# A gated recurrence followed by a two-matrix network: natural-order 64-column output tiles, whole loads of w_in, decays and operands one step ahead, three double-bank PSUM tiles

## The chip, the cores and the metric

The kernel runs on one core of a Trainium2 chip. The metric is device time in microseconds (us); the span that a profile shows is 1 to 2 us shorter. Runs called slow are left out of every comparison unless the text says so.

The engines are named as in the profile: PE is TensorE (PEld its weight loads), DVE is VectorE, ACT is ScalarE, POOL is GpSimd, SP issues the DMAs. `L142` is line 142 of the kernel that the profile belongs to.

## The reference

```python
batch, n_heads, seq, head_dim = (4, 8, 768, 48)
for t in range(S):                                     # _attn_ref(q, k, v, alpha)
    state = alpha[:, :, t, :, None] * state + np.einsum('bhd,bhe->bhde', k[:, :, t], v[:, :, t])
    y[:, :, t] = np.einsum('bhd,bhde->bhe', q[:, :, t], state)
# x = y as 3072 tokens x 384;  w_in is 384 x 2048, w_out is 2048 x 384
h = x @ w_in
g = h * np.cos(h)
out = g @ w_out
```

The inputs and the output are float32. The kernel works on 24 chunks of 128 tokens, six per batch entry, in bfloat16 with float32 sums.

## The kernel before

For each chunk the kernel does this, under the names that the text uses:

- **ln, sums, exps**: `ln` of alpha on ACT, cumulative sums by matmuls with a triangle of ones, then `exp(-sum)` (icp) and `exp(sum)` (cp) on ACT. All three are done for two chunks at a time.
- **operands**: POOL multiplies k by icp (khb) and q by cp (qhb), and casts v.
- **transposes** of khb and qhb on PE, evicted by DVE.
- **scores** (8 matmuls) with a mask on DVE; **state** (matmuls of khb and v plus the old state), evicted with the decay by DVE; **outputs** (old state and scores against v), evicted by DVE as the transposed x.
- **ff1**: 48 matmuls per chunk in two halves of 24. Each half fills one PSUM tile of two banks. ACT takes the cosine of the tile (`Sin` with a bias), and the **gate** on DVE multiplies.
- **ff2**: 16 matmuls, evicted by ACT and stored.

Step `s` of the loop runs ff1 of chunk `s`, ff2 of `s-1`, outputs of `s+1`, and transposes, state and scores of `s+2`. The order of instructions on each engine is the order of the program. The parts that matter, cut:

```python
    ps = ctx.enter_context(tc.tile_pool(name="ps", bufs=2, space=bass.MemoryType.PSUM))
    # tags: "big" [C,2,512] f32 = two banks (sums, scores, ff1); "g" one bank (transposes, state,
    # outputs); "o" one bank (ff2). Two buffers of each: 4 + 2 + 2 = 8 banks.

    def load_w1(f0, f1):                     # rows of w_in permuted to the order of outputs' rows
        w = moe_w_in[:, f0:f1].rearrange("(p a d) f -> a d p f", a=2, d=D)
        for i in range(2):
            nc.sync.dma_start(out=w1f[DA * i : DA * i + DA, :, f0:f1], in_=w[i, 0:DA, 0:3])
            nc.sync.dma_start(out=w1f[96:128, i, f0:f1], in_=w[i, 0:DA, 3])
        for i in range(2):
            o = 64 + DB * i
            nc.sync.dma_start(out=w1f[o : o + DB, :, f0:f1], in_=w[i, DA:D, 0:3])
            nc.sync.dma_start(out=w1f[o + 32 : o + 32 + DB, 2, f0:f1], in_=w[i, DA:D, 3])
    # ... cut ...
    # outputs(j): 28 matmuls into 32-column tiles, four of them side by side (16 in the first chunk
    # of a batch entry, where there is no state)
    # ... cut ...
    for s in range(NCH + 1):
        # ... loads for later steps, cut ...
        if s == 0:
            cums(2, 2); exps(2, 2); operands(2)
        elif s + 2 < NCH:
            operands(s + 2)
        if s + 2 < NCH:
            transposes(s + 2); ev_transposes(s + 2)
        if s < NCH:
            ff1(s, 0); t0 = act(s, 0)
        if s + 2 < NCH:
            state(s + 2); ev_state(s + 2)
        if s < NCH:
            gate(s, 0, t0)
        # ... casts of w_out in step 1, cut ...
        if s >= 1:
            ff2(s - 1, 0)
        if s < NCH:
            ff1(s, 1); t1 = act(s, 1)
        if s + 1 < NCH:
            outputs(s + 1); ev_outputs(s + 1)
        if s < NCH:
            gate(s, 1, t1)
        if s >= 1:
            ff2(s - 1, 1)
        if s + 2 < NCH:
            scores(s + 2); mask_scores(s + 2)
        if s % 2 == 0 and s + 4 < NCH:
            ln(s + 4, 2)
        if s % 2 == 1 and s + 3 < NCH:
            cums(s + 3, 2); exps(s + 3, 2)
        if s >= 1:
            ev_ff2(s - 1)
```

## Time and profile before

| what | value | where it is read |
|---|---|---|
| time, median of the first 3 runs | 290.99 us | times |
| span, mean granted TensorE clock | 289.8 us, 0.859 | cores |
| PE, DVE, ACT, POOL busy | 74, 48, 50, 26 % of the span | page, part 1 |
| DMA share, 0 to 50 us | 0.96 to 1.14 | windows of 10 us |
| ff1 of step 2 starts | 69.65 us | timeline |
| ff1 of step 20 starts, nine pairs of steps later | 256.66 us | timeline |
| table loads on ACT | 21+10+10+1 = 42, 1283 ns each | groups by line |

The page of the kernel before, part 2, cuts the span into 40 slices of 7.25 us. Digits are tenths (9 is 90% or more); the last row is GB/s.

```profile
PE   7402191695976958959949949959769769769995
PEclk9955568577997997998988979979969959979999
DMA  9999999904266157347525633642660650500001
GB/s 148 193 161 164 204 368 173 168 0 102 39 138 134 45 99 136 78 63 136 111 61 104 138 71 67 138 106 40 130 136 3 139 110 9 105 27 29 29 29 54
```

There are two regimes. For the first eight slices DMA is full and PE has little to do. DMA moves 148 to 204 GB/s while it loads w_in and the inputs, and 368 GB/s in the sixth slice, where w_out loads. From about 60 us on, PE is busy but for a dip every third slice or so, and the granted clock dips with it.

The waits of the kernel before say what the dip is (who waited for whom: us in total, times, longest):

```profile
POOL khb L184 <- ACT icp_new L172: 163.8, 12, 16.1
PE t L212 <- POOL khb L184: 50.7, 13, 9.1
PE t L212 <- POOL qhb L186: 4.9, 13, 0.6
```

And so does the chain of waits of the kernel before, in a window over one dip (start, duration, what):

```profile
105.79 0.09 PE cum_new L159 x4
...
106.09 1.15 issue
107.25 0.81 ACT icp_new L172
108.06 0.71 ACT cp_new L174
...
109.18 0.97 POOL qhb L186
110.15 0.05 issue
110.20 0.61 PE t L212 x4
110.81 2.32 PE t L320 x24
...
114.76 1.34 PE t L320 x24
```

The sums end, a table loads (the 1.15 us called issue), two exps run, POOL makes khb and qhb, and only then does PE transpose and start ff1. PE is idle for 3.4 us. Its next 24 ff1 matmuls take 2.32 us where the same 24 take 1.34 us later on: the granted clock is 0.50 to 0.60 over the first ff1 half after each of these dips. This comes once in two steps, ten times in all.

### The profile page before, as it was taken

What the parts mean: (1) busy time and instruction counts of PE and PEld (TensorE: products, weight loads), DVE (VectorE), ACT (ScalarE), POOL (GpSimd) and SP (SyncE); (2) the same over time, 40 slices, a digit from 0 to 9 for tenths busy, and PEclk for the clock granted to TensorE, in tenths of its full rate; (3) what the DMA queues carried; (4) which work ended last, traced back from release to release, by engine and by line L of the source; (5) the groups of instructions that cost most, each with busy time, mean ns of one, the idle gap of its engine ahead of it and who ended that gap; (6) DMA issues with size and microseconds to landing.
All of it is one profiled execution on the core that took longest, in us unless ns stands there. A gap on an engine that the chain in (4) does not pass through costs nothing.

```text
span 289.8 us, 6578 instructions
## 1 busy us (share of the span) xinstructions
PE 213.9 (74%) x2798; PEld 161.6 (56%) x2798; DVE 139.6 (48%) x162; ACT 145.8 (50%) x153; POOL 75.7 (26%) x178
## 2 busy tenths in 40 slices
PE   7402191695976958959949949959769769769995
PEld 2201081464755737738737747647557557557782
DVE  3333333651762653643735726717616616617651
ACT  4100345116755853863864666567555556553332
POOL 4131133007108007026034052071080080080000
PEclk9955568577997997998988979979969959979999
DMA  9999999904266157347525633642660650500001
GB/s 148 193 161 164 204 368 173 168 0 102 39 138 134 45 99 136 78 63 136 111 61 104 138 71 67 138 106 40 130 136 3 139 110 9 105 27 29 29 29 54
DMA packets 106463, 30.32 MB, mean 105 GB/s; under 512 B 100545, under 2 KB 105665, under 8 KB 106433
## 3 DMA queue, kind: packets, MB, share of 16 engines
q1 hardware_dynamic: 106432, 29.89, 52.5%
q8 instruction: 22, 0.36, 0.5%
q14 instruction: 9, 0.07, 0.1%
HBM read 25.17 MB, written 4.72 MB: 103 GB/s over the span
## 4 chain that ended last, share of the span: by engine, by line
PE 58%; SPq 9%; ACT 7%; DMA 7%; DVE 7%; issue 6%; POOL 4%; POOLq 0%; ACTq 0%; DVEq 0%
PE t L320 26%; PE o_new L343 18%; DVE g_new L334 5%; DMA w1f<-in_moe_w_in_dram 5%; PE t L212 4%; PE t L296 4%; POOL qhb L186 4%; ACT icp_new L172 3%; SPq L100 3%; ACT cp_new L174 2%; SPq L110 2%; DMA t<-in_k_dram 2%; SPq L105 2%; PE cum_new L155 2%; DVE t L304 2%
## 5 line engine op out<-in xcount | busy, mean ns | idle before, releaser
L329 ACT ACTIVATE c_sb<-t,halfpi 128x1024 bf16<-128x1024 f32 x48 | 53.5, 1114 | 81.7 <-PE t L320 81.5
L320 PE MATMUL t<-t,w_114 128*128 128x128 bf16 x1152 | 86.6, 242 | 0.1
L320 PEld LDWEIGHTS <-w_114 128*128 128x128 bf16 x1152 | 82.0, 111 | 3.9 <-issue 0.7
L343 PE MATMUL o_new<-w_116,g_new 128*128 128x384 bf16 x384 | 72.8, 335 | 2.7 <-DVE w_116 L136 2.7
L184 POOL TENSOR_TENSOR khb<-t,icp_new 128x384 bf16<-128x384 f32 x24 | 24.6, 1023 | 183.0 <-ACT icp_new L172 163.8
L334 DVE TENSOR_TENSOR g_new<-t,c_sb 128x1024 bf16<-128x1024 f32 x48 | 58.8, 1224 | 15.8 <-ACT c_sb L329 15.3
L343 PEld LDWEIGHTS <-g_new 128*128 128x128 bf16 x384 | 36.3, 100 | 27.0 <-issue 5.5
L212 PE MATMUL t<-ident_bf,khb 128*128 128x128 bf16 x96 | 12.0, 263 | 50.7 <-POOL khb L184 50.7
L218 DVE COPY t<-t 128x1024 bf16<-128x1024 bf16 x24 | 16.5, 687 | 60.1 <-PE t L212 60.1
L212 PEld LDWEIGHTS <-khb 128*128 128x128 bf16 x96 | 6.9, 114 | 53.4 <-POOL khb L184 52.3
L238 DVE TENSOR_TENSOR t<-t,mask_f 128x1024 bf16<-128x1024 f32 x24 | 29.3, 1223 | 0.0
L264 DVE TENSOR_TENSOR t<-t,Em 128x384 bf16<-128x384 f32 x24 | 13.4, 558 | 31.6 <-PE t L258 22.2
L329 ACT ACT_TABLE_LOAD x21 | 26.9, 1283 | 0.4
L304 DVE CAST t<-t 128x384 bf16<-128x384 f32 x24 | 13.4, 557 | 23.1 <-PE t L296 23.1
L186 POOL TENSOR_TENSOR qhb<-t,cp_new 128x384 bf16<-128x384 f32 x24 | 23.9, 998 | 0.1
L142 ACT ACTIVATE lnab<-a_new 128x768 bf16<-128x768 f32 (+1 forms) x13 | 10.3, 794 | 26.5 <-DMA a_new<-in_alpha_dram 24.7
L172 ACT ACT_TABLE_LOAD x10 | 12.8, 1283 | 20.7 <-PE cum_new L159 20.7
L155 PE MATMUL cum_new<-lnab,triu_bf 128*128 128x384 bf16 x24 | 7.7, 348 | 11.8 <-ACT lnab L142 10.1
L212 PE MATMUL t<-ident_bf,qhb 128*128 128x128 bf16 x96 | 12.2, 267 | 4.9 <-POOL qhb L186 4.9
L142 ACT ACT_TABLE_LOAD x10 | 12.8, 1283 | 3.4 <-DMA a_new<-in_alpha_dram 3.2
L296 PE MATMUL t<-t,vpb 128*32 128x128 bf16 x192 | 14.2, 219 | 0.0
L348 ACT ACTIVATE o_sb<-o_new 128x384 f32<-128x384 f32 x24 | 11.7, 487 | 5.0 <-PE o_new L343 5.0
(48 smaller groups left out, 184.2 us busy)
## 6 DMA issues: line engine op xcount, KB each, us to landing
a_new<-in_alpha_dram SPq DMA_DIRECT2D x24, 192.0 KB, 3.3
t<-in_k_dram SPq DMA_DIRECT2D x24, 192.0 KB, 3.7
t<-in_q_dram SPq DMA_DIRECT2D x24, 192.0 KB, 4.0
t<-in_v_dram SPq DMA_DIRECT2D x24, 192.0 KB, 4.1
out_dram<-o_sb SPq DMA_DIRECT2D x24, 192.0 KB, 2.0
w2f<-in_moe_w_out_dram SPq DMA_DIRECT2D x4, 768.0 KB, 8.9
w1f<-in_moe_w_in_dram SPq DMA_DIRECT2D x4, 384.0 KB, 6.6
w1f<-in_moe_w_in_dram SPq DMA_DIRECT2D x4, 192.0 KB, 9.2
```

The source lines that it names most:

```text
L142: nc.scalar.activation(out=lnab[:, g % 2, lo : lo + n, :, 0:D], in_=a_t[g][:, lo : lo + n], func=AF.Ln)
L172: nc.scalar.activation(out=icp_t[g][:, lo : lo + n], in_=cum_ps[g][:, lo : lo + n, 0:HD], func=AF.Exp, scale=-1.0)
L184: nc.gpsimd.tensor_tensor(out=khb[:, j % 2, :, 0:D], in0=k_sb, in1=icp.rearrange("s (h d) -> s h d", h=H), op=ALU.mult)
L186: nc.gpsimd.tensor_tensor(out=qhb[:, j % 2, :, 0:D], in0=q_sb, in1=cp[:, 0:HD].rearrange("s (h d) -> s h d", h=H), op=ALU.mult)
L212: nc.tensor.transpose(t[:, (i * NP + p) * C : (i * NP + p + 1) * C], src[:, j % 2, 2 * p : 2 * p + 2].rearrange("s h d -> s (h d)"), ident_bf)
L238: nc.vector.tensor_tensor(out=t.rearrange("s (h t) -> s h t", h=H), in0=A_ps.pop(j).rearrange("s (h t) -> s h t", h=H), in1=mask_f.unsquee ...
L296: nc.tensor.matmul(t[32 * qd : 32 * qd + 32, kt * C : (kt + 1) * C], w, m, start=(r == 0), stop=(r == len(mms[qd]) - 1), skip_group_check= ...
L304: nc.vector.tensor_copy(out=t.rearrange("r k t -> r (k t)"), in_=y_ps.pop(j)[:, 0 : 3 * C])
L320: nc.tensor.matmul(t[:, f], w1[:, kk, ft * C : (ft + 1) * C], x_t[j][:, kk], start=(kk == 0), stop=(kk == 2))
L329: nc.scalar.activation(out=c_sb, in_=t, func=AF.Sin, bias=halfpi, scale=1.0)
L334: nc.vector.tensor_tensor(out=g_t[j][:, half * HF : (half + 1) * HF], in0=t, in1=c_sb, op=ALU.mult)
L343: nc.tensor.matmul(o_ps[j][:, 0:DM], g_t[j][:, ft], w2[:, ft], start=(ft == 0), stop=(ft == NF - 1))
```

## The change

The intent: outputs come out in the natural order of the rows of x, in tiles of 64 columns, so that w_in loads in whole DMAs; decays and operands are prepared one step earlier; PSUM holds three double-bank tiles and one buffer each of the small ones. The core of the diff, cut:

```diff
-    ps = ctx.enter_context(tc.tile_pool(name="ps", bufs=2, space=bass.MemoryType.PSUM))
+    ps = ctx.enter_context(tc.tile_pool(name="ps", bufs=1, space=bass.MemoryType.PSUM))
     ... every tile of tag "big" gets bufs=3; khb and qhb get three slots instead of two
     def load_w1(f0, f1):
-        ... eight DMAs into 16 or 32 partitions
+        nc.sync.dma_start(out=w1f[:, :, f0:f1],
+                          in_=moe_w_in[:, f0:f1].rearrange("(k p) f -> p k f", p=C))
     def operands(j, qeng):
-        ... four POOL casts of v into vb and vpb
+        nc.gpsimd.tensor_copy(out=vpb[:, j % 3, :, 0:D], in_=v_sb)     # heads at stride 112, zeros between
     def outputs(j):
-        ... 28 matmuls into 32-column tiles
+        for kt in range(3):
+            if not first:
+                U = U_t[j - 1].rearrange("r p e -> r (p e)")
+                r = 0
+                while r < C:
+                    f = kt * C + r
+                    p = f // 96
+                    n = min(96 * (p + 1), (kt + 1) * C, f - f % 64 + 64) - f     # 64 or 32
+                    mm(r, n, kt, U[:, f : f + n], qT[:, (NP + p) * C : (NP + p + 1) * C], True, False)
+                    r += n
+            ... four 64-column matmuls of v against the scores
+    def prep(g):
+        cums(2 * g, 2)
+        exps(2 * g, 2)
+        if 2 * g + 2 < NCH:
+            ln(2 * g + 2, 2)
     for s in range(NCH + 1):
-        elif s + 2 < NCH:
-            operands(s + 2)
+        if s + 3 < NCH:
+            operands(s + 3, nc.gpsimd)
     ...
             ff2(s - 1, 1)
+            ev_ff2(s - 1)
     ...
         if s % 2 == 0 and s + 4 < NCH:
-            ln(s + 4, 2)
-        if s % 2 == 1 and s + 3 < NCH:
-            cums(s + 3, 2)
-            exps(s + 3, 2)
-        if s >= 1:
-            ev_ff2(s - 1)
+            prep(s // 2 + 2)
```

The casts of w_in also move in part from DVE to ACT, qhb of the first two chunks from POOL to DVE, inputs are loaded further ahead, the order of the start-up changes, and w_out loads in two DMAs instead of four.

More of the change, by code (lines that the diff above doesn't have):

```diff
@@ L36 @@
     HF = NF // 2
-    DA = 32
-    DB = D - DA
     HD = H * D
@@ L41 @@
     ACOL = [(h % 2) * NP + h // 2 for h in range(H)]
-    PF = 5
-    WARM = 30
+    PF = 6
+    VS = 112
     consts = ctx.enter_context(tc.tile_pool(name="consts", bufs=1))
-    apool = ctx.enter_context(tc.tile_pool(name="apool", bufs=3))
+    apool = ctx.enter_context(tc.tile_pool(name="apool", bufs=4))
     inpool = ctx.enter_context(tc.tile_pool(name="inpool", bufs=PF))
-    cpool = ctx.enter_context(tc.tile_pool(name="cpool", bufs=2))
+    cpool = ctx.enter_context(tc.tile_pool(name="cpool", bufs=3))
     work = ctx.enter_context(tc.tile_pool(name="work", bufs=2))
     moe = ctx.enter_context(tc.tile_pool(name="moe", bufs=2))
-    ps = ctx.enter_context(tc.tile_pool(name="ps", bufs=2, space=bass.MemoryType.PSUM))
+    ps = ctx.enter_context(tc.tile_pool(name="ps", bufs=1, space=bass.MemoryType.PSUM))
     ctx.enter_context(tc.manual_schedule())
@@ L68 @@
     make_identity(nc, ident_bf)
-    qhb = consts.tile([C, 2, H, 64], BF, tag="qhb")
-    khb = consts.tile([C, 2, H, 64], BF, tag="khb")
+    qhb = consts.tile([C, 3, H, 64], BF, tag="qhb")
+    khb = consts.tile([C, 3, H, 64], BF, tag="khb")
     nc.vector.memset(qhb, 0.0)
     nc.vector.memset(khb, 0.0)
-    vpb = consts.tile([C, 3, NP, 2, DA], BF, tag="vpb")
+    vpb = consts.tile([C, 3, H, VS], BF, tag="vpb")
     nc.vector.memset(vpb, 0.0)
@@ L76 @@
     make_upper_triangular(nc, mask_f, 1.0, diag=True)
-    m6 = consts.tile([C, 6], FP, tag="m6")
-    nc.vector.memset(m6, 0.0)
-    nc.vector.memset(m6[0:64, 0:2], 1.0)
-    nc.vector.memset(m6[0:64, 4:5], 1.0)
-    nc.vector.memset(m6[64:128, 2:4], 1.0)
-    nc.vector.memset(m6[64:128, 5:6], 1.0)
+    m2 = consts.tile([C, 2], FP, tag="m2")
+    nc.vector.memset(m2, 0.0)
+    nc.vector.memset(m2[0:64, 0:1], 1.0)
+    nc.vector.memset(m2[64:128, 1:2], 1.0)
     w1f = consts.tile([C, 3, DF], FP, tag="w1f")
@@ L113, in load_w1 @@
     def load_w1(f0, f1):
-        w = moe_w_in[:, f0:f1].rearrange("(p a d) f -> a d p f", a=2, d=D)
-        for i in range(2):
-            nc.sync.dma_start(out=w1f[DA * i : DA * i + DA, :, f0:f1], in_=w[i, 0:DA, 0:3])
-            nc.sync.dma_start(out=w1f[96:128, i, f0:f1], in_=w[i, 0:DA, 3])
-        for i in range(2):
-            o = 64 + DB * i
-            nc.sync.dma_start(out=w1f[o : o + DB, :, f0:f1], in_=w[i, DA:D, 0:3])
-            nc.sync.dma_start(out=w1f[o + 32 : o + 32 + DB, 2, f0:f1], in_=w[i, DA:D, 3])
+        nc.sync.dma_start(out=w1f[:, :, f0:f1],
+                          in_=moe_w_in[:, f0:f1].rearrange("(k p) f -> p k f", p=C))
     def cast_w1(f0, f1):
-        nc.vector.tensor_copy(out=w1[:, :, f0:f1], in_=w1f[:, :, f0:f1])
+        nc.scalar.activation(out=w1[:, 0:2, f0:f1], in_=w1f[:, 0:2, f0:f1], func=AF.Copy)
+        nc.vector.tensor_copy(out=w1[:, 2, f0:f1], in_=w1f[:, 2, f0:f1])
     def load_w2(f):
         nc.sync.dma_start(
-            out=w2f[:, f : f + 4],
-            in_=moe_w_out[f * C : (f + 4) * C, :].rearrange("(f p) n -> p f n", p=C),
+            out=w2f[:, f : f + 8],
+            in_=moe_w_out[f * C : (f + 8) * C, :].rearrange("(f p) n -> p f n", p=C),
         )
     def cast_w2(f):
-        nc.vector.tensor_copy(out=w2[:, f : f + 4], in_=w2f[:, f : f + 4])
+        nc.vector.tensor_copy(out=w2[:, f : f + 8], in_=w2f[:, f : f + 8])
     def ln(j0, n):
@@ L151, in cums @@
         if lo == 0 or n == 2:
-            cum_new = ps.tile([C, 2, 512], FP, tag="big")
+            cum_new = ps.tile([C, 2, 512], FP, tag="big", bufs=3)
             cum_ps[g] = cum_new
@@ L175, in exps, with operands @@
                              func=AF.Exp, scale=1.0)
-    Em_t, vb_t = {}, {}
-    def operands(j):
+    Em_t = {}
+    def operands(j, qeng):
         cp = cp_t[j // 2][:, j % 2]
@@ L183, in operands @@
         k_sb, q_sb, v_sb = k_t.pop(j), q_t.pop(j), v_t.pop(j)
-        nc.gpsimd.tensor_tensor(out=khb[:, j % 2, :, 0:D], in0=k_sb,
+        nc.gpsimd.tensor_tensor(out=khb[:, j % 3, :, 0:D], in0=k_sb,
                                 in1=icp.rearrange("s (h d) -> s h d", h=H), op=ALU.mult)
-        nc.gpsimd.tensor_tensor(out=qhb[:, j % 2, :, 0:D], in0=q_sb,
-                                in1=cp[:, 0:HD].rearrange("s (h d) -> s h d", h=H), op=ALU.mult)
-        vs = v_sb.rearrange("s (p a) d -> s p a d", a=2)
-        vb = work.tile([C, NP, 96], BF, tag="vb", bufs=3)
-        vb_t[j] = vb
-        nc.gpsimd.tensor_copy(out=vb[:, :, 0 : 2 * DA].rearrange("s p (a d) -> s p a d", a=2),
-                              in_=vs[:, :, :, 0:DA])
-        nc.gpsimd.tensor_copy(out=vb[:, :, 2 * DA : 96].rearrange("s p (a d) -> s p a d", a=2),
-                              in_=vs[:, :, :, DA:D])
-        for a in range(2):
-            nc.gpsimd.tensor_copy(out=vpb[:, j % 3, :, a, DB * a : DB * a + DB],
-                                  in_=vs[:, :, a, DA:D])
-        Em = work.tile([C, NP, 6], FP, tag="Em", bufs=3)
+        qeng.tensor_tensor(out=qhb[:, j % 3, :, 0:D], in0=q_sb,
+                           in1=cp[:, 0:HD].rearrange("s (h d) -> s h d", h=H), op=ALU.mult)
+        nc.gpsimd.tensor_copy(out=vpb[:, j % 3, :, 0:D], in_=v_sb)
+        Em = work.tile([C, NP, 2], FP, tag="Em", bufs=3)
         nc.gpsimd.tensor_tensor(
-            out=Em, in0=cp[:, HD:CW].unsqueeze(2).to_broadcast([C, NP, 6]),
-            in1=m6.unsqueeze(1).to_broadcast([C, NP, 6]), op=ALU.mult,
+            out=Em, in0=cp[:, HD:CW].unsqueeze(2).to_broadcast([C, NP, 2]),
+            in1=m2.unsqueeze(1).to_broadcast([C, NP, 2]), op=ALU.mult,
         )
@@ L213, in transposes @@
                     t[:, (i * NP + p) * C : (i * NP + p + 1) * C],
-                    src[:, j % 2, 2 * p : 2 * p + 2].rearrange("s h d -> s (h d)"), ident_bf)
+                    src[:, j % 3, 2 * p : 2 * p + 2].rearrange("s h d -> s (h d)"), ident_bf)
     def ev_transposes(j):
@@ L223, in scores @@
     def scores(j):
-        t = ps.tile([C, H * C], FP, tag="big")
+        t = ps.tile([C, H * C], FP, tag="big", bufs=3)
         A_ps[j] = t
@@ L253, in state @@
                 t[:, p * 96 : (p + 1) * 96],
-                khb[:, j % 2, 2 * p : 2 * p + 2].rearrange("s h d -> s (h d)"),
-                vb_t[j][:, p], start=(p == 0), stop=first, skip_group_check=True,
+                khb[:, j % 3, 2 * p : 2 * p + 2].rearrange("s h d -> s (h d)"),
+                vpb[:, j % 3, 2 * p : 2 * p + 2, 0:D], start=(p == 0), stop=first, skip_group_check=True,
             )
@@ L264, in ev_state @@
         nc.vector.tensor_tensor(
-            out=t.rearrange("r p (u e) -> r p u e", u=6),
-            in0=U_ps.pop(j)[:, 0 : NP * 96].rearrange("r (p u e) -> r p u e", p=NP, u=6),
-            in1=Em_t.pop(j).unsqueeze(3).to_broadcast([C, NP, 6, DB]), op=ALU.mult,
+            out=t.rearrange("r p (a e) -> r p a e", a=2),
+            in0=U_ps.pop(j)[:, 0 : NP * 96].rearrange("r (p a e) -> r p a e", p=NP, a=2),
+            in1=Em_t.pop(j).unsqueeze(3).to_broadcast([C, NP, 2, D]), op=ALU.mult,
         )
@@ L276, in outputs, with mm @@
         first = j % NC == 0
-        for kt in range(3):
-            mms = []
-            for qd in range(4):
-                p, i = (kt, qd) if qd < 3 else (3, kt)
-                a = []
-                if not first:
-                    a.append((U_t[j - 1][:, p, DA * i : DA * (i + 1)],
-                              qkT_t[j][:, (NP + p) * C : (NP + p + 1) * C]))
-                if i < 2:
-                    hs = [(2 * p + i, vb_t[j][:, p, DA * i : DA * (i + 1)])]
-                else:
-                    hs = [(2 * p + e, vpb[:, j % 3, p, e]) for e in range(2)]
-                for h, w in hs:
-                    a.append((w, A_t[j][:, ACOL[h] * C : (ACOL[h] + 1) * C]))
-                mms.append(a)
-            for r in range(max(len(a) for a in mms)):
-                for qd in range(4):
-                    if r < len(mms[qd]):
-                        w, m = mms[qd][r]
-                        nc.tensor.matmul(
-                            t[32 * qd : 32 * qd + 32, kt * C : (kt + 1) * C], w, m,
-                            start=(r == 0), stop=(r == len(mms[qd]) - 1),
-                            skip_group_check=True,
-                        )
+        vs = vpb[:, j % 3].rearrange("s h e -> s (h e)")
+        qT = qkT_t[j]
+        def mm(r0, n, kt, lhsT, rhs, start, stop):
+            nc.tensor.matmul(t[r0 : r0 + n, kt * C : (kt + 1) * C], lhsT, rhs, start=start,
+                             stop=stop, skip_group_check=True)
+        for kt in range(3):
+            if not first:
[5 more added lines that the diff above has]
+                    n = min(96 * (p + 1), (kt + 1) * C, f - f % 64 + 64) - f
+                    mm(r, n, kt, U[:, f : f + n], qT[:, (NP + p) * C : (NP + p + 1) * C],
+                       True, False)
+                    r += n
+            for r in range(2):
+                for half in range(2):
+                    T = 2 * kt + half
+                    g, sl = T // 3, 2 * (T % 3) + r
+                    h = 4 * g + (sl + 1) // 2
+                    c0 = 4 * VS * g + 64 * sl
+                    mm(64 * half, 64, kt, vs[:, c0 : c0 + 64],
+                       A_t[j][:, ACOL[h] * C : (ACOL[h] + 1) * C], first and r == 0, r == 1)
     def ev_outputs(j):
@@ L307, in ev_outputs @@
         A_t.pop(j)
-        vb_t.pop(j)
         U_t.pop(j - 1, None)
@@ L314, in ff1 @@
     def ff1(j, half):
-        t = ps.tile([C, HF, C], FP, tag="big")
+        t = ps.tile([C, HF, C], FP, tag="big", bufs=3)
         h_ps[j, half] = t
@@ L360 @@
     load_qk(0)
+    load_v(0)
     load_a(1)
-    load_v(0)
     load_w1(0, DF // 2)
@@ L370 @@
     load_v(2)
-    for f in range(0, NF, 4):
-        load_w2(f)
     load_a(4)
     load_a(5)
+    load_w2(0)
+    load_w2(8)
     load_qk(3)
     load_v(3)
+    load_a(6)
+    load_a(7)
+    load_qk(4)
+    load_v(4)
     ln(0, 1)
@@ L382 @@
     ln(1, 1)
-    operands(0)
-    warmup(6)
+    operands(0, nc.vector)
+    warmup(4)
     transposes(0)
@@ L388 @@
     exps(1, 1)
+    scores(0)
+    mask_scores(0)
+    warmup(4)
     state(0)
     ev_state(0)
-    scores(0)
-    mask_scores(0)
-    cast_w1(0, DF // 2)
-    warmup(6)
     outputs(0)
     ev_outputs(0)
-    operands(1)
+    cast_w1(0, DF // 2)
+    operands(1, nc.vector)
+    warmup(8)
     transposes(1)
     ev_transposes(1)
+    ln(2, 2)
     state(1)
     ev_state(1)
-    ln(2, 2)
     scores(1)
     mask_scores(1)
-    cast_w1(DF // 2, DF)
+    prep(1)
+    operands(2, nc.gpsimd)
     for s in range(NCH + 1):
-        if s + 6 < NCH:
-            load_a(s + 6)
-        if s + 4 < NCH:
-            load_qk(s + 4)
-            load_v(s + 4)
-        if s == 0:
-            cums(2, 2)
-            exps(2, 2)
-            operands(2)
-        elif s + 2 < NCH:
-            operands(s + 2)
+        if s + 8 < NCH:
+            load_a(s + 8)
+        if s + 5 < NCH:
+            load_qk(s + 5)
+            load_v(s + 5)
+        if s + 3 < NCH:
+            operands(s + 3, nc.gpsimd)
         if s + 2 < NCH:
@@ L431 @@
             gate(s, 0, t0)
+        if s == 0:
+            cast_w1(DF // 2, DF)
         if s == 1:
-            for f in range(0, NF, 4):
+            for f in range(0, NF, 8):
                 cast_w2(f)
```

## The prediction

> **What bounds the kernel now.** Two regimes.
>
> 1. Start-up, to about 50 us: DMA. In the table of 10 us windows its share is 0.96 to 1.14, while TensorE is busy 1.5 to 4.2 us per window from 10 to 50. Bytes move at 148 to 204 GB/s while w_in (16 DMAs into 16 or 32 partitions) and 192-byte rows load, but at 368 GB/s in the slice (36 to 43 us) where w_out loads into 128 partitions.
> 2. Then a cycle of two steps, 20.45 us. In the chain of waits each odd step ends in cumulative sums, a table load (1.28), two exps (0.81, 0.72), POOL khb and qhb (1.0 each), and only then transposes and ff1. The timeline shows TensorE idle 3.4 us there, then at clock 0.50 for about 3.5 us: the first ff1 half takes 2.3 us, not 1.34. Agrees with the Trainium skill, "TensorE: Matmul & The Clock Gate", Part 1: half clock after an idle window of about 3.4 us. Ten gaps, about 5 us each.
>
> **What changes.**
> - Decays and operands run a step ahead: the exp-POOL-transpose wait leaves the path, with it the clock drop. TensorE's work for two steps at full clock, from the chain: about 15.1 us (ff1 1.34 x4, ff2 1.30 x4; transposes 0.55, scores 0.4, state 0.35, outputs 0.6, x2 each; sums 0.5).
> - But exps and ln now stand together on ScalarE before the next Sin, and the built program still loads a table between exp and ln: 1.28+0.81+0.72+1.28+0.84+1.28 = 6.2 us after the sums before the next cosine. The skill, "ScalarE: Activation LUTs", What ACT_TABLE_LOAD costs, gives 1283 ns; so does the trace.
> - The small PSUM tile is now single-buffered. The next transposes wait until the outputs are evicted, which in-order VectorE does only after the gate behind that cosine. cosine ends 7.4 us after the sums, gate 8.7, eviction 9.25; TensorE reaches those transposes at 7.25: idle 2.0. Then gate 10.45, mask 11.65, transposes' eviction 12.35; TensorE wants the state at 11.25: idle 1.1. No wait follows; sums end at 18.2. With latency, estimate 18.5 us per pair. Both idle stretches are under 3.4 us, so the clock should stay full.
> - Outputs: 20 matmuls, 64 or 32 columns wide, not 28; still 0.6 us.
> - w_in in two whole DMAs: at w_out's rate 3.1 MB takes about 8.5 us instead of 18. Ln of chunks 6 and 7 now blocks ScalarE until its load lands, about 43 us; first ff2 at about 50 us instead of 56.6, ff1 of step 2 at 57 instead of 69.9.
>
> **Sum.** 57 + nine pairs of 18.5 (before 20.45) + the tail from step 20, unchanged at 36: span 259.5, time about 260 us (before 291), range 245 to 275. Chances: faster by over 2% 0.97, within 2% 0.02, slower 0.01.
>
> **What would show it.**
> - Granted clock near 1.00 in steady state, ff1 halves about 1.34 us; waits for POOL (55 us) gone.
> - Transposes wait for the outputs' eviction (about 2 us per pair), the state for the transposes' eviction (about 1), both behind the cosine.
> - Table loads fall from 42 to 31.
> - Over 300 GB/s while w_in loads; first ff2 near 50 us.
>
> **What would make it wrong.** Single-buffered tiles stall more than laid out and the half clock stays (275 or more); w_in moves no faster (+8); wide outputs run one after another (+0.4 per pair); or stalls overlap better, pairs near 16 us (240).

## The result and the profile after

The changed kernel takes 261.9 us (median of 4 runs, 260.5 to 262.83), the kernel before 291.3 us (median of 4 runs, 290.19 to 293.11). The ratio is 0.898, 95% interval 0.892 to 0.904. Ratios in this document are the mean time of one kernel's fast runs over the mean of the other's fast runs of the same rounds, so they are not quite the ratio of the medians quoted.

The page of the changed kernel, part 2 (slices of 6.5 us):

```profile
PE   7661673399969969969969869879789699999994
PEclk9775779689999979999999999999999989999998
DMA  8999999907734843743762671664355140000001
GB/s 142 314 300 188 347 238 179 197 5 154 152 74 84 155 99 53 154 107 60 141 133 59 115 151 41 113 146 93 69 123 116 39 92 33 33 2 31 33 30 62
```

While w_in loads (the second and third slices) DMA now moves 300 to 314 GB/s, and the clock row is 9 nearly everywhere after the start. The waits of the changed kernel:

```profile
PE t L192 <- DVE t L287: 14.6, 8, 2.3
PE o_new L325 <- DVE w_114 L125: 8.0, 1, 8.0
PE t L232 <- DVE t L198: 6.7, 8, 0.9
PE t L192 <- POOL khb L173: 2.5, 3, 2.0
```

L192 is the transposes, L287 the eviction of the outputs, L232 the state, L198 the eviction of the transposes. PE's 55.6 us of waiting for POOL have become 3.4 us (2.5 for khb and 0.9 for qhb). Two new waits stand in their place, 21.3 us together. The timeline of the changed kernel over one pair shows where they come from (start, duration, engine, line, work, then in brackets the idle time before it):

```profile
122.65 0.24 PE L148 MATMUL cum_new<-ones_bf,lnab 128*128 128x1 bf16 x4
122.97 1.28 ACT L161 ACT_TABLE_LOAD   x1 [0.49 <-PE cum_new L148]
...
125.81 1.28 ACT L131 ACT_TABLE_LOAD   x1
127.10 0.84 ACT L131 ACTIVATE lnab<-a_new 128x768 bf16<-128x768 f32 x1
...
127.96 1.28 ACT L311 ACT_TABLE_LOAD   x1
...
129.25 2.12 ACT L311 ACTIVATE c_sb<-t,halfpi 128x1024 bf16<-128x1024 f32 x2
...
130.40 1.22 DVE L316 TENSOR_TENSOR g_new<-t,c_sb 128x1024 bf16<-128x1024 f32 x1 [4.70 <-ACT c_sb L311]
...
131.54 0.55 DVE L287 CAST t<-t 128x384 bf16<-128x384 f32 x1
...
132.14 0.38 PE L192 MATMUL t<-ident_bf,khb 128*128 128x128 bf16 x4 [1.55 <-DVE t L287]
...
135.01 0.34 PE L232 MATMUL t<-vpb,khb 128*128 128x96 bf16 x4 [0.92 <-DVE t L198]
```

After the sums ACT runs a table load, two exps, a second table load, ln, a third table load, and only then the cosine. DVE waits for the cosine, and behind that gate in its queue stands the eviction of the outputs, which frees the only small PSUM tile. So PE waits 1.55 us before the transposes and 0.92 us before the state.

Where the 29.6 us of span (289.8 to 260.2) came from, by the starts of ff1 in the two timelines:

| stretch | before | after | gain |
|---|---|---|---|
| start to ff1 of step 2 | 69.65 | 57.87 | 11.8 |
| ff1 of step 2 to ff1 of step 20 (nine pairs) | 187.0 (20.8 a pair) | 167.3 (18.6 a pair) | 19.7 |
| from there to the end | 33.1 | 35.1 | -1.9 |

Two of the first ff1 halves still run at a low clock in the profiled run: those of step 6 and step 18, 2.49 and 2.77 us by the timeline, where 1.50 is usual in that view. The idle before each was 2.27 and 2.28 us. An equal gap of 2.28 us at step 12 was followed by full clock, and so were the five gaps of 1.55 us. The timeline of the changed kernel shows the transposes behind the gap and the ff1 half after them, at steps 6, 12 and 18:

```profile
93.95 0.38 PE L192 MATMUL t<-ident_bf,khb 128*128 128x128 bf16 x4 [2.27 <-DVE t L287]
94.39 2.49 PE L302 MATMUL t<-t,w_112 128*128 128x128 bf16 x24
...
150.77 0.38 PE L192 MATMUL t<-ident_bf,khb 128*128 128x128 bf16 x4 [2.28 <-DVE t L287]
151.22 1.50 PE L302 MATMUL t<-t,w_112 128*128 128x128 bf16 x24
...
206.99 0.38 PE L192 MATMUL t<-ident_bf,khb 128*128 128x128 bf16 x4 [2.28 <-DVE t L287]
207.51 2.77 PE L302 MATMUL t<-t,w_112 128*128 128x128 bf16 x24
```

The clock records of the traces explain the difference. In every trace here the granted clock changes only at points that lie a multiple of 3.41 us apart. In this trace it is 0.50 from 94.69 to 98.10 us and from 207.33 to 210.74 us. The gaps of steps 6 and 18 each lie inside one stretch of 3.41 us that ends at 94.69 or 207.33 us. The gap of step 12 (148.49 to 150.77 us) is cut by the point at 149.30 us into 0.81 and 1.47 us. The profiles of twelve fast runs, from step 2 to step 22, agree: of 563 such stretches at full clock with at most 1.63 us of idle on PE (between the modelled ends and the next starts), none was followed by half clock, and of 30 with 2.11 us or more, all were. Between 1.78 and 2.06 us it was nine of eleven.

### The profile page after: what moved, and what is told of

Its sections match the earlier page's. It is cut to its first block, busy times and chain, and to the rows that moved or that the text cites. A ratio compares the mean times of both kernels' runs of the same rounds, so it can differ in the third digit from the quotient of the medians.

```text
span 260.2 us, 6131 instructions
## 1 busy us (share of the span) xinstructions
PE 211.3 (81%) x2625; PEld 155.4 (60%) x2626; DVE 136.1 (52%) x160; ACT 135.6 (52%) x144; POOL 62.6 (24%) x104
## 5 line engine op out<-in xcount | busy, mean ns | idle before, releaser
L311 ACT ACTIVATE c_sb<-t,halfpi 128x1024 bf16<-128x1024 f32 x48 | 52.5, 1112 | 71.2 <-PE t L302 71.1
L316 DVE TENSOR_TENSOR g_new<-t,c_sb 128x1024 bf16<-128x1024 f32 x48 | 58.5, 1218 | 49.9 <-ACT c_sb L311 49.9
L302 PE MATMUL t<-t,w_112 128*128 128x128 bf16 x1152 | 77.4, 227 | 3.2 <-ACT w_112 L115 3.2
L325 PE MATMUL o_new<-w_114,g_new 128*128 128x384 bf16 x384 | 71.9, 332 | 8.6 <-DVE w_114 L125 8.0
L302 PEld LDWEIGHTS <-w_112 128*128 128x128 bf16 x1152 | 72.4, 103 | 6.9 <-ACT w_112 L115 3.5
L287 DVE CAST t<-t 128x384 bf16<-128x384 f32 x24 | 13.3, 554 | 32.8 <-PE t L261 32.8
L330 ACT ACTIVATE o_sb<-o_new 128x384 f32<-128x384 f32 x24 | 11.8, 490 | 23.3 <-PE o_new L325 23.3
L192 PE MATMUL t<-ident_bf,khb 128*128 128x128 bf16 x96 | 9.6, 223 | 17.1 <-DVE t L287 14.6
L198 DVE COPY t<-t 128x1024 bf16<-128x1024 bf16 x24 | 16.4, 682 | 9.9 <-PE t L192 9.9
L261 PE MATMUL t<-t 128*64 128x128 bf16 (+1 forms) x160 | 20.8, 231 | 0.0
L261 PE MATMUL t<-t,vpb 128*64 128x128 bf16 x288 | 18.9, 228 | 0.7 <-DVE t L244 0.7
L192 PEld LDWEIGHTS <-khb 128*128 128x128 bf16 x96 | 6.4, 99 | 19.4 <-issue 14.7
L161 ACT ACT_TABLE_LOAD x10 | 12.8, 1283 | 4.5 <-PE cum_new L148 4.4
L261 PEld LDWEIGHTS <-t 128*64 128x64 bf16 (+1 forms) x160 | 10.4, 100 | 6.7 <-issue 0.2
L311 ACT ACT_TABLE_LOAD x11 | 14.1, 1283 | 0.2
L232 PE MATMUL t<-vpb,khb 128*128 128x96 bf16 x96 | 8.7, 216 | 6.7 <-DVE t L198 6.7
```

The source lines that it names most:

```text
L192: nc.tensor.transpose(t[:, (i * NP + p) * C : (i * NP + p + 1) * C], src[:, j % 3, 2 * p : 2 * p + 2].rearrange("s h d -> s (h d)"), ident_bf)
L198: nc.vector.tensor_copy(out=t, in_=qkT_ps.pop(j))
L261: nc.tensor.matmul(t[r0 : r0 + n, kt * C : (kt + 1) * C], lhsT, rhs, start=start, stop=stop, skip_group_check=True)
L287: nc.vector.tensor_copy(out=t.rearrange("r k t -> r (k t)"), in_=y_ps.pop(j)[:, 0 : 3 * C])
L302: nc.tensor.matmul(t[:, f], w1[:, kk, ft * C : (ft + 1) * C], x_t[j][:, kk], start=(kk == 0), stop=(kk == 2))
L311: nc.scalar.activation(out=c_sb, in_=t, func=AF.Sin, bias=halfpi, scale=1.0)
```

## The experiments

The theory after the result had three parts. (1) Running ahead gives the gain of the steady pairs. (2) Whole loads of w_in give the gain of the start-up. (3) What is left between PE's own work and the 18.6 us of a pair is set by ACT's run of table loads in front of the cosine, and by slower outputs. The rivals were that the third big PSUM tile carries the change, that the order of loads gives the start-up, and that the single small PSUM tile sets the new waits whatever ACT does.

| run | median us | ratio to before | start of ff1, steps 2 and 20 |
|---|---|---|---|
| b_wwhole | 281.3 | 0.962 | 59.25, 246.10 |
| b_ahead | 268 (mean of 3 fast runs) | 0.913 | not used, slow profile |
| a_noahead | 295.6 | 1.010 | 58.78, 257.50 |
| a_wsplit | 271.5 | 0.925 | 69.17, 236.75 |
| a_psum222 | 263.1 | 0.899 | 57.79, 226.88 |
| a_pad64 | 256.0 | 0.876 | 57.91, 221.84 |
| a_lnfirst | 259.8 | 0.888 | 61.13, 223.48 |
| best1 | 254.2 | 0.869 | not used |
| best2 | 249.5 | 0.853 | 60.67, 215.41 |
| a_onetable | 243.6 | 0.831 | 56.09, 207.01 |
| best3 | 235.6 | 0.802 | not used, slow profile |
| best5 | 233.1 | 0.796 | 56.18, 199.18 |

The kernel before had a median of 292.8 to 293.7 us in the rounds of these runs. All results were correct but those of b_wwhole and a_wsplit.

### b_wwhole: w_in whole, in the kernel before

```diff
-        ... eight DMAs
+        nc.sync.dma_start(out=w1f[:, :, f0:f1],
+                          in_=moe_w_in[:, f0:f1].rearrange("(k p) f -> p k f", p=C))
```

> The kernel before with only the w_in load changed to two whole DMAs (rows land in an order that its outputs do not have, so the result is wrong on purpose). My theory: the start-up part of the gain is the rate of w_in; at w_out's rate it takes 8.5 us instead of 18, so 281 to 285 us, and the steady cycle of 20.45 us per pair is untouched. Rival, that the start-up gain comes from the order of loads and from running ahead: 289 to 292.

Measured: 281.3 us, as expected. ff1 of step 2 starts at 59.25 us instead of 69.65, and the nine pairs after it take 186.9 us against 187.0. The whole gain lies in the start-up. While w_in loads (7 to 28 us) DMA moves 280 GB/s, against 176 in the same stretch of the kernel before.

### a_wsplit: w_in split again, in the changed kernel

```diff
-        nc.sync.dma_start(out=w1f[:, :, f0:f1], ...)
+        ... the eight DMAs of before
```

> The changed kernel with w_in loaded as before, in 16 small DMAs (rows in the wrong order for it, so the result is wrong on purpose). My theory: about the 11.8 us that whole loads gave the kernel before are lost again, 270 to 276 us. Rival, that the other changes of the start-up (order of loads, running ahead) carry the gain and w_in is hidden: 262 to 266.

Measured: 271.5 us, as expected. ff1 of step 2 starts at 69.17 us, within half a microsecond of the kernel before. So running ahead and the new order of loads bring next to nothing to the start-up; w_in is nearly all of it. Whether the size of the DMAs or the number of partitions that each one writes makes the difference was not tried apart.

### b_ahead: decays and operands ahead, in the kernel before

```diff
+        if s + 3 < NCH:
+            operands(s + 3)          # three slots of khb and qhb; sums, exps, ln at the end of even steps
```

As in the changed kernel, inputs are loaded further ahead and `ev_ff2` moves ahead of the scores in this run.

> The kernel before with only decays and operands moved one step ahead (three slots of khb and qhb, sums, exps and ln at the end of even steps); split w_in, 32-column outputs and two buffers of every PSUM tile stay. My theory: running ahead alone removes the wait of transposes on POOL and the half clock, pair near 18.5 us: 268 to 275. Rival, that the third double-bank PSUM tile is what makes running ahead pay: 283 or more, with ff1 or scores waiting for a big tile.

Measured: 266.5, 267.9 and 270.1 us in its fast runs, ratio 0.913; two more runs were slow. That is at the lower edge of the first theory and far from the rival's 283. So running ahead is worth more than the rest of the change together, with two big tiles and 32-column outputs. The profile fell in a slow run, so only the kind of wait is taken from it: PE's scores wait there for a gate to free a big tile (23.5 us in 9 places). That is the rival's mechanism, but it doesn't eat the gain.

### a_noahead: the changed kernel without running ahead

```diff
-        if s + 3 < NCH:
-            operands(s + 3, nc.gpsimd)
+        if s == 0:
+            cums(2, 2); exps(2, 2); operands(2, nc.gpsimd)
+        elif s + 2 < NCH:
+            operands(s + 2, nc.gpsimd)
     ... ln, cums, exps and ev_ff2 at the end of the step as before
```

> The changed kernel with decays and operands put back to where before has them. My theory: the 3.4 us idle and the half clock return in ten places, pair near 20.5 to 21 us: 278 to 285. Rival, that the gain is start-up and layout: 262 to 266.

Measured: 295.6 us, 1.0% above the kernel before and outside both ranges. The half clock did return (the granted clock over nine pairs is 0.89, against 0.98 in the changed kernel), and so did the idle, as the waits of this run show:

```profile
PE t L192 <- POOL khb L173: 37.5, 13, 3.4
PE t L192 <- POOL qhb L175: 5.1, 12, 0.6
```

But nine pairs take 198.7 us, 11.7 more than in the kernel before, which gives back all that whole loads gain. Something else in the new layout costs time in every pair. Part of it is the outputs: they take 1.19 us with a state, against about 0.61 before. Fifteen of the 18 chunks in nine pairs have a state, and 15 x 0.58 is 8.7 us (an estimate from the two timelines; here no idle stands behind the outputs to absorb it). The other 3 us are probably half clock that lasted longer: over the nine pairs the mean granted clock is 0.886 against 0.902 in the kernel before, which withholds 22.6 us of full clock instead of 18.4 (an estimate from the clock records).

### a_psum222: two buffers of every PSUM tile in the changed kernel

```diff
-    t = ps.tile([C, H * C], FP, tag="big", bufs=3)
+    t = ps.tile([C, H * C], FP, tag="big")            # and the pool with bufs=2
```

> The changed kernel with PSUM buffers as before (two of each tile). My theory: the third big tile is not needed; the wait for the outputs' eviction goes, a wait of scores for the gate's big tile comes: 258 to 266. Rival, that the third tile carries the change: 270 or more.

Measured: 263.1 us, ratio 0.899 against 0.898: in this kernel it makes no difference to the time whether PSUM holds a third big tile or second small ones. The wait only changes its place. The line below is from the waits of this run; L209 is the scores, L316 the gate:

```profile
PE t L209 <- DVE g_new L316: 11.2, 8, 1.9
```

No wait of the transposes for the outputs' eviction is left in this run, but scores wait for a big tile. Both waits end with a gate that stands behind the late cosine.

### a_pad64: every output matmul 64 columns wide

```diff
+    upad = consts.tile([C, 3, NP, 128], BF, tag="upad")       # the state at stride 128, zeros between
-                    mm(r, n, kt, U[:, f : f + n], ...)                    # n is 64 or 32
+                    mm(64 * half, 64, kt, U[:, c0 : c0 + 64], ..., st[half], False)
```

> The changed kernel with the state kept at a stride of 128 with zeros, so that every output matmul is 64 columns wide. My theory: the outputs' 1.18 us falls to about 0.65 because the 32-column pieces cost about 0.28 us for each change of width. Only every second chunk's outputs lie on the path, so 255 to 259 us; the other's gain becomes idle time before the transposes (1.55 to about 2.1 us), and if that idle halves the clock as the two gaps of 2.3 us did, 260 to 270. Rival, that the number of matmuls sets the time: outputs stay at 1.18 and the time at 262.

Measured: 256.0 us, within the range. There are 20 matmuls per chunk with a state in both versions, but the stretch from the outputs' first matmul to ff2's falls from 1.19 to 0.69 us. The two ends of that stretch, from the timeline of the changed kernel:

```profile
127.60 0.41 PE L261 MATMUL t<-t 128*64 128x128 bf16 x3
...
128.79 1.47 PE L325 MATMUL o_new<-w_114,g_new 128*128 128x384 bf16 x8
```

And from the timeline of a_pad64:

```profile
117.98 0.25 PE L263 MATMUL t<-t,upad 128*64 128x128 bf16 x2
...
118.67 1.15 PE L326 MATMUL o_new<-w,g_new 128*128 128x384 bf16 x6
```

(The view calls the first group by its first shape; of the three matmuls of the changed kernel, two are 32 columns wide.) The four changes between 64 and 32 columns therefore cost about 0.5 us, 0.12 us each, less than half of the 0.28 us that was expected for each. That it is the changes, and not the narrow matmuls, can be read from the trace of the changed kernel. There a matmul of the outputs starts 0.15 to 0.17 us after the one before it at each change of width (at 127.78, 127.94, 128.34 and 128.50 us in this chunk; 72 changes after 60 us are all alike), and at most 0.08 us after it where the width stays. The 28 matmuls of the kernel before, all 32 wide, take only 0.61 us. The Trainium skill says as much in "TensorEngine Tiling (Array Packing)", Key Properties: changing the tiling mode drains the engine. It gives no number.

### a_lnfirst: ln before the exps

```diff
     def prep(g):
         cums(2 * g, 2)
-        exps(2 * g, 2)
         if 2 * g + 2 < NCH:
             ln(2 * g + 2, 2)
+        exps(2 * g, 2)
```

> The changed kernel with ln issued before the exps in each preparation. My theory: one table load fewer per pair (21 instead of 31) and ln runs during the sums, so the cosine comes about 2 us earlier and the idle of 1.55 us before the transposes nearly goes; the wait of the state (0.9 us) stays. Pair 18.6 to about 17.1, 245 to 252 us. Rival, that the single small PSUM tile and not ScalarE sets the idle: 259 or more.

Measured: 259.8 us. That lies in the rival's range (259 or more), but it decides nothing, since the premise of the edit failed, as the timeline of this run shows:

```profile
123.73 1.28 ACT L131 ACT_TABLE_LOAD   x1
125.02 0.84 ACT L131 ACTIVATE lnab<-a_new 128x768 bf16<-128x768 f32 x1
125.89 1.28 ACT L161 ACT_TABLE_LOAD   x1
127.18 0.81 ACT L161 ACTIVATE icp_new<-cum_new 128x768 f32<-128x768 f32 x1
```

The compiled program still loads a table between ln and exp, whichever comes first: 31 loads as before, not 21. The cosine came only about 0.5 us earlier, and the idle before the transposes fell from 1.55 to 1.07 us, by as much. Nine pairs took 162.4 us instead of 167.3, without any half clock (granted 1.00 against 0.98), but ff1 of step 2 came 3.3 us later: ln stands first in the start-up too and waits there for its load (ACT is idle for 4.80 us before the ln at 28.40 us). So the total hides most of the gain. The steady part agrees with theory (3) in size, but it took a cleaner run.

### a_onetable: one table for exp and ln

```diff
     def prep(g):
+        nc.scalar.preload_act_table_set("natural_log_exp_and_others")
         cums(2 * g, 2)
```

> The changed kernel with one line more: each preparation first loads the table set that has both exp and ln, so the loads fall from 31 to 23, and the load no longer waits for the sums. My theory, that the cosine behind this run of ScalarE work sets both idle stretches of TensorE: it comes 2.56 us earlier, the 1.55 us before the transposes go and about 0.6 of the 0.9 before the state, pair 18.6 to about 16.5: 240 to 248 us. Rival, that the single small PSUM tile sets them whatever ScalarE does: 257 or more. (The run with ln first could not tell: it kept 31 loads.)

Measured: 243.6 us, 18 us faster than the changed kernel by one line. There are 23 table loads, and nine pairs take 150.9 us, 16.8 a pair. That is 16.4 us less; 13.5 us of it is the wait below, and most of the rest is half clock that no longer comes (granted 1.00 between steps 2 and 20, against 0.98). The small tile still has one buffer. These are the waits of this run that answer to the two new ones of the changed kernel:

```profile
PE t L232 <- DVE t L198: 6.6, 9, 0.9
PE t L192 <- DVE t L287: 1.1, 3, 0.4
```

The wait before the transposes is nearly gone with the single tile in place, so ACT's run of work set it, and the rival falls. Before the state most pairs still wait; the expectation that 0.6 us of that would go was wrong. The Trainium skill, "ScalarE: Activation LUTs", Table sets, says that ln and exp share a set and need one load.

### best1, best2, best3, best5: the parts together

best1 is a_lnfirst and a_pad64 together; best2 adds two buffers of every PSUM tile; best3 adds the table set of a_onetable; best5 adds two edits of the start-up:

```diff
     def prep(g):
+        # in the first two preparations exps before ln, later ln before exps
-            for f in range(0, NF, 8):
-                cast_w2(f)
+            cast_w2(0)
+            nc.scalar.activation(out=w2[:, 8:16], in_=w2f[:, 8:16], func=AF.Copy)
```

> Both: ln first and all outputs 64 wide, three big PSUM tiles. The two gains should add, since ln first takes away the idle into which the shorter outputs would fall: pair about 16.3, 238 to 246 us.

> As the run with ln first and 64-wide outputs, but two buffers of each PSUM tile. If small tiles still stall there: 2 to 6 us faster than with three big tiles; if a big tile is what is short: slower by as much.

> Two buffers of every PSUM tile, 64-wide outputs, ln first, and the one table set. Its kin without the table set took 249.5 us, with TensorE waiting 0.8 us per pair for the exps' big tile and 0.65 for the second gate's. Both sit behind the same ScalarE run and should go: pair 17.4 to about 16, 234 to 241 us.

> As the run with two buffers of every PSUM tile, 64-wide outputs, ln first and one table set (235.6 us), with two start-up edits: in the first two preparations exps stand before ln again, because there ln waits for a load and held ff1 of step 0 back to 33.0 us against 27.5 in the changed kernel; and ScalarE casts the second half of w_out beside VectorE. If those waits bound the start-up: ff1 of step 2 at 57 to 58 us instead of 60.9 and 231 to 234 us. If loads bound it whatever the order: no change, 235 to 237. The pair stays at about 16.0 in both.

best1 missed its range (254.2 us), since it rested on the same failed premise as a_lnfirst. best2 was 4.7 us faster than best1: in this version two small tiles are better than a third big one. best3 was 235.6 us (one of its four runs, the profiled one, was slow), and its kin best5 233.1 us, ratio 0.796 with a 95% interval of 0.789 to 0.803 (the verdict printed with best5 was "unclear", for a reason that I don't know; it is correct and its four runs lie between 232.8 and 234.0 us). In best5 nine pairs take 143.0 us, 15.9 a pair, and ff1 of step 2 starts at 56.2 us, a little earlier than expected. The steady wait of PE left there is for a gate, 3.4 us in 8 places. The page of best5:

```profile
PE   7770557479999999999999999999999999999993
PEclk9796577758999999999999999999999999999999
```

From the tenth slice on PE is at 9 up to the last slice, and the clock from the eleventh. What is left is mostly PE's own work and some 55 us of start-up.

## Why the prediction was right

**What bounds the kernel now.** Right in both regimes. b_wwhole and a_wsplit show the start-up part by itself, b_ahead and a_noahead the pair part.

**Running ahead frees the transposes and the clock.** Right: waits for POOL 55.6 to 3.4 us, most ff1 halves 1.34 us. b_ahead shows that this alone gives a ratio of 0.913.

**Three table loads in one run before the cosine, and two new idle stretches behind it.** Right, down to the queue: laid out as 2.0 and 1.1 us, measured as 1.55 and 0.92, and 31 loads as counted. a_onetable shows that the ACT run is the cause of the first and larger one.

**18.5 us per pair.** Measured 18.6. It was right partly because two errors met. "Outputs: 20 matmuls, 64 or 32 columns wide, not 28; still 0.6 us" was wrong: 1.19 us with a state. The prediction counted matmuls and left out the drains at each change of width, though it listed slow outputs as a risk of 0.4 us per pair. For the chunk whose outputs stand ahead of the transposes' wait, the extra 0.58 us fell into that idle time, which is why it was 1.55 us and not 2.0. The other chunk's 0.58 us went into the pair, and about made up the allowance for latency.

**"Both idle stretches are under 3.4 us, so the clock should stay full."** This step failed. Where the outputs had no state, the idle was 2.3 us, and two of those three gaps were followed by half clock. The length of a gap is not what decides here: in these traces it is the idle within one stretch of 3.41 us, and about 1.8 to 2.1 us of it were enough. It cost 1.0 and 1.3 us in these halves (2.49 and 2.77 us instead of 1.50 for 24 matmuls) and at most 1.7 us each in all (half of 3.41 us), too little to see in the total.

**w_in at w_out's rate.** Right in the time: about 10 us expected, 10.4 us in b_wwhole, 11.3 us the other way in a_wsplit. The rate itself stayed below w_out's: 300 to 314 GB/s in the slices, against 368.

**First ff2 at 50, ff1 of step 2 at 57.** Measured 49.9 and 57.9. That ln of chunks 6 and 7 would hold ACT until about 43 us was right too; it started at 43.26 us. The tail was called unchanged at 36; it was 33.1 before and 35.1 after. So the prediction took a tail that was 2.9 us too long and missed that it would grow by 1.9 us; that the two nearly cancel is luck. In a_pad64 the tail is 34.1, so the slower outputs are about half of the growth; the rest was not traced.

What the prediction did not see is that the parts don't add. From the ratios, running ahead alone gives 8.7% and w_in alone 3.8%, together more than the whole change (10.2%). The difference is 2.3%, or 6.7 us. In a_pad64 the state's wider matmuls return 5.9 us, so the narrow pieces are probably most of it; that they are is inferred from the sizes. The one profile of b_ahead, a slow run, doesn't show it: a pair takes 18.6 us there too.

## What to carry to other kernels

When a wait is taken off the critical path, lay out the queues again with what moved: here the gain of running ahead was cut by table loads that had come to stand in one run, and one line that named a shared table set was worth 18 us. Cost narrow matmuls by how often the tile width changes and not by their number alone. When idle time can't be avoided, look at how much of it falls together in time, as the clock here answered to that and not to a single gap's length. A change of several parts should be split in both directions, since one part (here the new layout) can cost time and hide behind the others.

## What the Trainium skill lacked or had wrong

- "TensorE: Matmul & The Clock Gate", Part 1, ties the half clock to an idle window of about 3.4 us. Here 2.27 and 2.28 us of idle were followed by half clock in two of three places, and 1.55 us in none of five. The page does say that the window runs freely, and elsewhere that frequent short idles can suffice; what share of a window suffices is not said there. In twelve fast runs here it was all of 30 stretches of 3.41 us with 2.11 us of idle or more, and none of 563 with 1.63 us or less.
- "TensorEngine Tiling (Array Packing)", Key Properties, says that changing the tiling mode drains TensorE, without a cost. Four changes between 64 and 32 columns cost about 0.5 us here (1.19 against 0.69 us for 20 matmuls each), 0.12 us each.
- "ScalarE: Activation LUTs", Table sets, gives ln then exp as one load. Both orders compiled to two loads here (31 in all) until the kernel named the shared set (23); the page's rules say to use the shared set, but not that the kernel has to ask for it by name.
- "ScalarE: Activation LUTs", What ACT_TABLE_LOAD costs, adds a drain of about 1380 ns to the 1283 ns of a load. Here the next activation starts 0.01 to 0.02 us after the load ends (122.97 + 1.28, then 124.27 us in the changed kernel), so a switch cost about 1.3 us.
